# Linear attention in two-batch or one-batch units, ahead of a top-1 mixture of experts and a feed-forward layer

## The chip, the cores and the metric

One core of a Trainium2 chip runs the whole program. The metric is the device time of one execution in microseconds (us). The core's engines are TensorE (PE, matmuls; its weight loads are PEld), VectorE (DVE), ScalarE (ACT), GpSimd (POOL) and SyncE (SP, which here issues DMAs). Each works through its own queue in program order and waits on semaphores; transfers run on 16 DMA engines.

## The reference, cut to what matters

```python
# q, k, v: (8 batches, 8 heads, 576 positions, 64), f32
q_s = exp(q - max(q, axis=-1));  q_s = q_s / (sum(q_s, axis=-1) + 1e-9)
k_s = exp(k - max(k, axis=2));   k_s = k_s / (sum(k_s, axis=2) + 1e-9)   # axis 2: positions
kv  = einsum('bhsd,bhse->bhde', k_s, v)
x   = einsum('bhsd,bhde->bhse', q_s, kv)      # -> (4608 tokens, 512)
# then: x through one of 8 experts per token, picked by argmax(x @ w_gate):
#   gate * sigmoid(x @ w_output_gate) * (relu(x @ w1[e]) @ w2[e])
# then: h = x @ w_in;  out = (h * cos(h)) @ w_out
```

## The kernel before

The program has three stages: attention, the experts, the feed-forward layer. Only attention is touched.

Attention works in eight **units** w = 0 to 7 of four heads for two batches: unit w belongs to the pair of batches u = w // 2 and to its lower or upper four heads (n = w % 2). Lower partitions (0 to 63) hold the pair's first batch, upper ones (64 to 127) the second; a partition holds nine positions of each head, as `[128, 4 heads, 9, 64]`. Each of k, q and v is loaded by `load` in two DMAs, one for each half of the partitions (unit 0's k in four). All of them stand in SP's queue, with the stores of finished tiles (`xs`) between them. There are three buffers for k, two for q and two for v.

For k: VectorE takes the maximum over the nine positions in a partition (`k_max`, L368, two halves); TensorE transposes it (`k_T`), VectorE reduces again (`k_red`), TensorE spreads the result over the partitions (`k_bc`) and ScalarE copies it out (`k_cp`, tile bc). GpSimd subtracts it from k (`k_sub`, L393; unit 0 on VectorE), ScalarE takes the exponential (`k_exp`, L397), and TensorE multiplies k by v with a column of ones (`kv_mm`, L435). VectorE divides by the sum (`kv_fin`) into one of two tiles bd. From that, TensorE, with a transposition (`kv_T`) and a copy by ScalarE (`kv_cp`, tile bT, L456), works out the columns for the router's logits (`kv_w`, `kv_wc`).

For q: VectorE takes the maximum over 64 (`q_max`, L408), GpSimd subtracts it in place (`q_sub`, L412), and ScalarE takes the exponential into a tile e of the pair, `[128, 9, 8 heads, 64]` (`q_exp`, L418). There are two buffers of e; a pair's exponential waits until the last tile of two pairs ago has been transposed.

A pair has nine **tiles** i of 128 tokens, 36 in all. For each, TensorE transposes e (`x_T`, L473), ScalarE copies the result out of PSUM (`x_cp`, L477, tile qT), TensorE multiplies by bd (`x_mm`, L485), and ScalarE copies the product out in two pieces (`x_st`, L492 and L493). After each third tile VectorE takes reciprocals (`x_rec`), GpSimd scales the logits (`x_lt`, L508), VectorE sums them (`x_lg`), and SP stores the three tiles into xs. After nine tiles VectorE finds each token's expert (`argmax`, L520 to L528) and gate (`gate`).

When 27 tiles are done, the tokens for the first expert are ranked (`rank_cnt` to `first_idx`) and gathered from xs by GpSimd (L280), scaled, transposed (`trans0`, L627) and split into a high and a low part (`xhigh` L297, `xlow` L302). Meanwhile the first expert's weights are loaded (tile raw), cast by ScalarE (wh, L267) and subtracted (wl, L271) into space that attention's loads held until then. The first expert product is L1171.

`keep_clock` (L211) issues matmuls whose result nobody reads, at five places: at the start (30), ahead of the first k-v product (16), of the first expert's number (16), of the ranking (20), and ahead of the two transpositions in `trans0` (26 and 30).

What sets the order: `issue` gets each step with a key and the steps it depends on, and writes out the ready step with the least key. The key is a base time plus a number from the table `SHIFT`, one number a step and unit.

Of the kernel before, what the change touches and what calls it, by code (L numbers as in the profile page):

```python
# [60 lines left out]
def kernel(  # L61
# [21 lines left out]
    NT = N // 128  # L83
# [221 lines left out]
    with ExitStack() as actx:  # L305
# [34 lines left out]
        KEEP = {("kv", 0): 16, ("first",): 16, ("rk0",): 20}  # L340
# [4 lines left out]
        def hpair(m):  # L345
            return slice(2 * m, 2 * m + 2)

# [7 lines left out]
        def load(nm, pool, src, w):  # L355
            u, n = w // 2, w % 2
            t = V[nm, w] = pool.tile([128, HH, C, D], F32, tag=nm, name=nm)
            parts = 1 if w or nm != "k" else 2
            for m in range(parts):
                hs = slice(HH // parts * m, HH // parts * (m + 1))  # L360
                for b in range(2):
                    sy.dma_start(out=t[64 * b:64 * b + 64, hs], in_=src[2 * u + b, HH * n:HH * n + HH, :, :][hs].rearrange(
                        "h (p c) d -> p h c d", c=C))

        def k_max(w, m):
            if ("m1", w) not in V:
                V["m1", w] = ap2.tile([128, HH, D], F32, tag="m1", name="m1")
            ve.tensor_reduce(out=V["m1", w][:, hpair(m)], in_=V["k", w][:, hpair(m)].rearrange("p h c d -> p h d c"), axis=AX, op=ALU.max)  # L368
# [58 lines left out]
        def kv_mm(w, m):  # L427
# [3 lines left out]
            for c in range(C):  # L431
                for o in range(2):
                    for b in range(2):
                        pr = slice(64 * b, 64 * b + 64)
                        pe.matmul(kvp(w)[64 * o:64 * o + 64, b, m, :], V["k", w][pr, 2 * m + o, c, :], v1t[w % 2][pr, 2 * m + o, c, :],  # L435
# [22 lines left out]
        def kv_w(w):  # L458
            for b in range(2):
                for m in range(2):  # L460
                    for o in range(2):
                        pr = slice(64 * o, 64 * o + 64)
                        pe.matmul(kvw(w)[pr, b, m, :], V["bT", w][:, b, m, pr], wgo[:, HH * (w % 2) + 2 * m + o, :], start=True, stop=True)
# [11 lines left out]
        def x_cp(i):  # L475
            t = V["qT", i] = ap3.tile([128, NP, 128], F32, tag="qT", name="qT")
            sc.copy(out=t, in_=V["qp", i])  # L477

        def x_mm(i):
            xp = V["xp", i] = ps_x.tile([128, 2, NP, 128], F32, tag="x", name="xp")  # L480
            for j in range(NP):
                for o in range(2):
                    for b in range(2):
                        pr, rows = slice(64 * o, 64 * o + 64), slice(64 * b, 64 * b + 64)
                        pe.matmul(xp[rows, o, j, 0:BD], V["qT", i][pr, j, rows], bdt[i // C % NBD][pr, b, j, :], start=True, stop=True)  # L485

        def x_st(i, u):
# [4 lines left out]
            sc.copy(out=V["xt", i - u][:, u, :, 0:2 * D].rearrange("p j (o d) -> p o j d", o=2), in_=xp[:, :, :, 0:D])  # L492
            sc.copy(out=V["xl", i - u][:, u].rearrange("p j o g -> p o j g"), in_=xp[:, :, :, D:BD])  # L493
# [126 lines left out]
        def trans0(a):  # L620
# [4 lines left out]
            keep_clock(t.rearrange("p d c -> p (d c)"), (26, 30)[a])  # L625
# [20 lines left out]
        for w in range(NW):  # L646
# [9 lines left out]
            o("ldq", -8, lambda w=w: load("q", qp, q, w), ("qexp0", w - QB), ("qexp1", w - QB))  # L656
# [11 lines left out]
            for m in range(2):  # L668
                o(f"qsub{m}", 10 + 2 * m, lambda w=w, m=m, en=en: q_sub(w, m, en[f"qsub{m}"]), ("qmax", w))
# [1121 lines left out]
```

## Time and profile before

| | |
|---|---|
| median of 3 runs | 1466.26 us (1463.46 to 1467.59) |
| profiled execution | 1464.81 us |
| its span | 1462.6 us |
| TensorE busy | 1377.8 us (94%) |
| VectorE busy | 944.5 us (65%) |
| ScalarE busy | 860.6 us (59%) |
| GpSimd busy | 542.8 us (37%) |
| first expert product (L1173) | at 216.07 us of the span |

The profile gives, for one execution, what each engine did in each stretch of the span, what ended each idle time, and the chain of work that ended last. A busy share is a mean over stages, so the stretch that the change touches has to be asked for by itself. Times inside the span count from its start; 2.2 us of the profiled time lie outside it.

### The profile page before, as it was taken

What the parts mean: (1) busy time and instruction counts of PE and PEld (TensorE: products, weight loads), DVE (VectorE), ACT (ScalarE), POOL (GpSimd) and SP (SyncE); (2) the same over time, 40 slices, a digit from 0 to 9 for tenths busy, and PEclk for the clock granted to TensorE, in tenths of its full rate; (3) what the DMA queues carried; (4) which work ended last, traced back from release to release, by engine and by line L of the source; (5) the groups of instructions that cost most, each with busy time, mean ns of one, the idle gap of its engine ahead of it and who ended that gap; (6) DMA issues with size and microseconds to landing.
All of it is one profiled execution on the core that took longest, in us unless ns stands there. A gap on an engine that the chain in (4) does not pass through costs nothing.

```text
span 1462.6 us, 27860 instructions
## 1 busy us (share of the span) xinstructions
PE 1377.8 (94%) x10855; PEld 1223.6 (84%) x10855; DVE 944.5 (65%) x1415; ACT 860.6 (59%) x1561; POOL 542.8 (37%) x385
## 2 busy tenths in 40 slices
PE   4667589999999999999999999999999999999998
PEld 3455479899998999898898888988889898898986
DVE  5568659677887788876655655546565554655543
ACT  2456533555665656566766656666666666666654
POOL 3465532564635454625152423406042240603000
PEclk7588779999999999999999999999999999999999
DMA  9998533777988788897667675766667566665662
GB/s 207 222 247 216 176 125 123 250 254 255 343 283 300 269 282 296 280 315 251 219 188 217 175 229 167 213 191 195 207 168 232 171 203 201 196 203 171 205 177 82
DMA packets 164748, 318.15 MB, mean 218 GB/s; under 512 B 15040, under 2 KB 22720, under 8 KB 164608
## 3 DMA queue, kind: packets, MB, share of 16 engines
q1 hardware_dynamic: 133952, 263.12, 60.0%
q10 hardware_dynamic: 24656, 33.33, 6.2%
q0 software_dynamic: 6000, 19.83, 4.2%
q8 instruction: 88, 1.44, 0.4%
q14 instruction: 52, 0.43, 0.1%
HBM read 264.17 MB, written 52.05 MB: 216 GB/s over the span
## 4 chain that ended last, share of the span: by engine, by line
PE 83%; DVE 6%; DMA 5%; ACT 4%; issue 2%; SPq 0%; ACTq 0%; DVEq 0%
PE acc L1662 8%; PE acc L1660 8%; PE acc L1661 8%; PE bank L1596 7%; PE bank L1598 7%; PE bank L1597 7%; PE hp L1171 6%; PE hp L1174 6%; PE yps L1209 5%; PE yps L1208 5%; PE yps L1207 5%; PE hp L1173 4%; DMA k<-in_k_dram 2%; DMA v<-in_v_dram 2%; DVE n L1630 1%
## 5 line engine op out<-in xcount | busy, mean ns | idle before, releaser
L1596 PE MATMUL bank<-xo,wp 128*128 128x256 f32 x994 | 281.4, 283 | 2.1 <-ACT part L1610 0.6
L1597 PE MATMUL bank<-xo,wp 128*128 128x256 f32 x994 | 277.2, 279 | 0.6 <-DVE xo L887 0.6
L1598 PE MATMUL bank<-xo,wp 128*128 128x256 f32 x994 | 277.4, 279 | 0.0
L1639 DVE SCALAR_TENSOR_TENSOR n<-n,h 128x512 f32<-128x512 f32 x144 | 125.9, 874 | 171.3 <-ACT n L1636 171.3
L1660 PE MATMUL acc<-wh,ht 128*128 128x512 f32 x576 | 227.6, 395 | 0.4 <-ACT ht L1645 0.4
L1661 PE MATMUL acc<-wl,ht 128*128 128x512 f32 x576 | 227.4, 395 | 0.0
L1662 PE MATMUL acc<-wh,ht 128*128 128x512 f32 x576 | 226.8, 394 | 0.2 <-DVE ht L1649 0.2
L1596 PEld LDWEIGHTS bank<-xo,wp 128*128 128x128 f32 x994 | 186.8, 188 | 23.1 <-ACT part L1610 4.2
L1597 PEld LDWEIGHTS bank<-xo,wp 128*128 128x128 f32 x994 | 186.7, 188 | 17.1 <-DVE xo L887 0.8
L1171 PE MATMUL hp<-xTh,wh 128*128 128x256 f32 x704 | 190.6, 281 | 0.5 <-ACT xTh L297 0.5
L1174 PE MATMUL hp<-xTh,wl 128*128 128x256 f32 x704 | 188.8, 278 | 0.0
L1598 PEld LDWEIGHTS bank<-xo,wp 128*128 128x128 f32 x994 | 187.3, 188 | 0.0
L271 DVE TENSOR_TENSOR wl<-raw,wh 128x1024 fp32r<-128x1024 f32 x121 | 171.6, 1448 | 13.1 <-ACT wh L267 12.3
L887 POOL TENSOR_TENSOR xo<-x,xo 128x512 fp32r<-128x512 f32 x24 | 31.2, 1298 | 372.7 <-ACT xo L882 372.7
L1618 DVE TENSOR_TENSOR h<-bank,part 128x256 f32<-128x256 f32 x213 | 89.1, 420 | 110.6 <-PE bank L1598 109.8
L267 ACT CAST wh<-raw 128x1024 fp32r<-128x1024 f32 x126 | 126.8, 1051 | 54.5 <-PE yps L1209 35.7
L1173 PE MATMUL hp<-xTl,wh 128*128 128x256 f32 x544 | 151.5, 278 | 0.3 <-DVE xTl L302 0.3
L1625 ACT ACTIVATE n<-h 128x512 int32<-128x512 f32 x144 | 91.1, 633 | 101.9 <-DVE h L1618 98.1
L1633 ACT ACTIVATE n<-n 128x512 f32<-128x512 f32 x144 | 91.2, 633 | 77.4 <-DVE n L1630 77.3
L1171 PEld LDWEIGHTS hp<-xTh,wh 128*128 128x128 f32 x704 | 132.3, 188 | 1.8 <-ACT xTh L297 0.6
L1174 PEld LDWEIGHTS hp<-xTh,wl 128*128 128x128 f32 x704 | 132.2, 188 | 0.2
L1662 PEld LDWEIGHTS acc<-wh,ht 128*128 128x128 f32 x576 | 108.3, 188 | 26.3 <-DVE ht L1649 1.0
(290 smaller groups left out, 2977.6 us busy)
## 6 DMA issues: line engine op xcount, KB each, us to landing
wp<-ws SPq DMA_DIRECT2D x504, 256.0 KB, 2.8
raw<-in_moe_w_dram SPq DMA_DIRECT2D x60, 1024.0 KB, 7.5
ws<-wst ACTq DMA_DIRECT2D x28, 512.0 KB, 4.6
ys<-yt ACTq DMA_DIRECT2D x39, 256.0 KB, 4.8
xs<-xt SPq DMA_DIRECT2D x12, 780.0 KB, 5.0
v<-in_v_dram SPq DMA_DIRECT2D x16, 576.0 KB, 15.9
q<-in_q_dram SPq DMA_DIRECT2D x16, 576.0 KB, 13.2
out_dram<-o SPq DMA_DIRECT2D x35, 256.0 KB, 2.9
```

The costliest lines, as they stand in the source:

```text
L267: sc.copy(out=wh[j, c][:, s], in_=rawt[c][:, s])
L271: eng.tensor_tensor(out=wl[j, c][:, s], in0=rawt[c][:, s], in1=wh[j, c][:, s], op=ALU.subtract)
L1171: pe.matmul(hp[:, f2, :], w_h, xTh[j][:, d, :], start=(d == 0), stop=False)
L1173: pe.matmul(hp[:, f2, :], w_h, xTl[j][:, d, :], start=False, stop=False)
L1174: pe.matmul(hp[:, f2, :], w_l, xTh[j][:, d, :], start=False, stop=(d == KD - 1))
L1596: pe.matmul(h, w[:, 0, k], x[:, i, 0, k], start=(first and k == 0), stop=False, skip_group_check=True)
L1597: pe.matmul(h, w[:, 0, k], x[:, i, 1, k], start=False, stop=False, skip_group_check=True)
L1598: pe.matmul(h, w[:, 1, k], x[:, i, 0, k], start=False, stop=(k == 1), skip_group_check=True)
L1639: ve.scalar_tensor_tensor(out=rs[j, s], in0=rs[j, s], scalar=-0.5, in1=hs[j, s], op0=ALU.add, op1=ALU.mult)
L1660: pe.matmul(acc[t, a], gh[f][:, ts], w_h, start=(c == 0), stop=False)
L1661: pe.matmul(acc[t, a], gh[f][:, ts], w_l, start=False, stop=False)
L1662: pe.matmul(acc[t, a], gl[f][:, ts], w_h, start=False, stop=(c == KF - 1))
```

## The change

A unit w is now one batch with all its eight heads. Lower partitions hold its even heads, upper ones its odd heads; a pair u still has two units, its two batches. Since heads follow each other in memory, `load` now moves a unit with one DMA over all 128 partitions (unit 0's k with two). The four slots j of a unit are its four pairs of heads, and half m of a unit is the slots m and m + 2 (`spair`), so that columns of e, rows of bd and the logits' weights are picked in a new pattern; the tiles in xs are the same rows and columns as before.

`q_exp` goes. `q_sub` writes its difference into e, and `x_cp` takes the exponential while it copies the transposed tile out of PSUM. So the wait for a free e, which was ScalarE's, is GpSimd's.

`keep_clock` loses the 16 and the 20 ahead of the first expert's number and of the ranking; the 26 and 30 become 10 and 10. All numbers in `SHIFT` for attention are new.

```diff
-        KEEP = {("kv", 0): 16, ("first",): 16, ("rk0",): 20}
+        KEEP = {("kv", 0): 16}
...
+        def spair(m):
+            return slice(m, HH, 2)
...
         def load(nm, pool, src, w):
-            u, n = w // 2, w % 2
             t = V[nm, w] = pool.tile([128, HH, C, D], F32, tag=nm, name=nm)
+            rows = src[w].rearrange("h s d -> (h s d)").rearrange("(j p f) -> p j f", p=128, f=C * D)
             parts = 1 if w or nm != "k" else 2
             for m in range(parts):
-                hs = slice(HH // parts * m, HH // parts * (m + 1))
-                for b in range(2):
-                    sy.dma_start(out=t[64 * b:64 * b + 64, hs], in_=src[2 * u + b, HH * n:HH * n + HH, :, :][hs].rearrange(
-                        "h (p c) d -> p h c d", c=C))
+                js = slice(m, HH, parts)
+                sy.dma_start(out=t[:, js].rearrange("p j c d -> p j (c d)"), in_=rows[:, js])
...
         def q_sub(w, m, eng):
-            t = V["q", w][:, hpair(m)]
-            eng.tensor_tensor(out=t, in0=t, in1=V["qm", w][:, hpair(m)].unsqueeze(3).to_broadcast([128, 2, C, D]), op=ALU.subtract)
-
-        def q_exp(w, m):
             u, n = w // 2, w % 2
             if ("e", u) not in V:
                 V["e", u] = (ep if u % 2 else rp1).tile([128, C, H, D], F32, tag="e", name="e")
-            sc.activation(out=V["e", u].rearrange("p c h d -> p h c d")[:, HH * n + 2 * m:HH * n + 2 * m + 2], in_=V["q", w][:, hpair(m)],
-                          func=AF.Exp)
+            out_ = V["e", u].rearrange("p c h d -> p h c d")[:, HH * n + 2 * m:HH * n + 2 * m + 2]
+            eng.tensor_tensor(out=out_, in0=V["q", w][:, spair(m)], in1=V["qm", w][:, spair(m)].unsqueeze(3).to_broadcast([128, 2, C, D]),
+                              op=ALU.subtract)
...
-            sc.copy(out=t, in_=V["qp", i])
+            sc.activation(out=t, in_=V["qp", i], func=AF.Exp)
...
-            keep_clock(t.rearrange("p d c -> p (d c)"), (26, 30)[a])
+            keep_clock(t.rearrange("p d c -> p (d c)"), (10, 10)[a])
...
-            xl1={(0,): 55.71},
+            xl1={(0,): 49.31},
```

How the change moves instructions is shown at three places. Tiles carry their numbers there, so that two of one name can be told apart.

SP's queue at the start, before (each row an issue with the partitions and sizes of its target):

```order
L362 DMA k_215<-in_k_dram 64x2x576 x4
L362 DMA v_223<-in_v_dram 64x4x576 x2
L362 DMA q_231<-in_q_dram 64x4x576 x2
L362 DMA k_301<-in_k_dram 64x4x576 x2
L362 DMA v_326<-in_v_dram 64x4x576 x2
L362 DMA q_331<-in_q_dram 64x4x576 x2
```

and of the change:

```order
L364 DMA k_215<-in_k_dram 128x2x576 x2
L364 DMA q_224<-in_q_dram 128x4x576
L364 DMA k_238<-in_k_dram 128x4x576
L364 DMA v_261<-in_v_dram 128x4x576
L364 DMA q_267<-in_q_dram 128x4x576
L364 DMA k_274<-in_k_dram 128x4x576
```

Each pair of issues has become one, and q comes ahead of v.

GpSimd's queue around the units 5 to 7, before (L393 subtracts from k, L412 from q, L508 scales logits):

```order
L412 TENSOR_TENSOR q_953<-q_953,qm_1175 128x1152 x2
L543 IOTA ci_1242 128x512
L544 IOTA cj_1243 128x512
L393 TENSOR_TENSOR k_844<-k_844,bc_1125 128x1152 x2
L508 TENSOR_TENSOR xl_1129<-xl_1129,xt_1128 128x24x16
L412 TENSOR_TENSOR q_1290<-q_1290,qm_1454 128x1152 x2
L508 TENSOR_TENSOR xl_1281<-xl_1281,xt_1280 128x24x16
L393 TENSOR_TENSOR k_1042<-k_1042,bc_1623 128x1152 x2
```

and of the change (L394 subtracts from k, L416 from q into e):

```order
L416 TENSOR_TENSOR e_910<-q_1132,qm_1134 128x2x9x64
L416 TENSOR_TENSOR e_1410<-q_1263,qm_1265 128x2x9x64
L508 TENSOR_TENSOR xl_1144<-xl_1144,xt_1143 128x24x16
L394 TENSOR_TENSOR k_1007<-k_1007,bc_1515 128x2x576 x2
L508 TENSOR_TENSOR xl_1303<-xl_1303,xt_1302 128x24x16
L508 TENSOR_TENSOR xl_1414<-xl_1414,xt_1413 128x24x16
L394 TENSOR_TENSOR k_1581<-k_1581,bc_1701 128x2x576
L508 TENSOR_TENSOR xl_1663<-xl_1663,xt_1662 128x24x16
```

The first write into the last pair's e (e_1410) now stands ahead of both subtractions from the k of the units 6 and 7.

ScalarE's queue from the last exponential of k on, before (L267 casts expert weights, L456 copies bT, L477 copies a transposed tile):

```order
L397 ACTIVATE k_1354<-k_1354 128x1152
L267 CAST wh_2126<-raw_2112 128x1024
L267 CAST wh_2131<-raw_2124 128x1024 x2
L196 ACTIVATE d_2146<-d_2146 128x72
L201 ACTIVATE s_2151<-s_2151 128x9
L477 COPY qT_2184<-qp_1993 128x512
L267 CAST wh_2191<-raw_2129 128x1024 x2
L477 COPY qT_2208<-qp_2186 128x512
L477 COPY qT_2215<-qp_2210 128x512
L456 COPY bT_2246<-bp_2241 64x512
```

and of the change:

```order
L398 ACTIVATE k_1581<-k_1581 128x2x576
L267 CAST wh_2081<-raw_2060 128x1024
L267 CAST wh_2084<-raw_2072 128x1024 x2
L267 CAST wh_2081<-raw_2060 128x1024
L454 COPY bT_2102<-bp_2076 64x512
L475 ACTIVATE qT_2171<-qp_1985 128x512
L267 CAST wh_2195<-raw_2074 128x1024 x2
L475 ACTIVATE qT_2199<-qp_2173 128x512
L475 ACTIVATE qT_2206<-qp_2201 128x512
```

bT moved from behind five casts, the gate's two exponentials and three tiles to behind four casts.

## Rows read from the trace of the kernel before

**Rows 1.** The page's 40 equal slices of the span: busy share of the DMA engines in tenths.
```profile
DMA  9998533777988788897667675766667566665662
```

**Rows 2.** Stretches: length, each engine's busy us (instructions), granted clock, DMA share, GB/s.
```profile
10.00:40.00 30.00, 11.59 (x179) 8.25 (x179) 16.43 (x15) 7.51 (x8) 10.79 (x5) 0.68 1.05 222
40.00:70.00 30.00, 20.64 (x345) 16.31 (x346) 14.33 (x14) 13.85 (x21) 13.26 (x6) 0.56 1.05 222
234.00:240.00 6.00, 6.00 (x28) 4.93 (x27) 5.62 (x18) 0.95 (x3) 0.01 (x1) 1.00 1.05 396
```

**Rows 3.** DMA issues up to 216 us: count, KB each, median us to landing.
```profile
v<-in_v_dram SPq DMA_DIRECT2D x16, 576.0 KB, 15.9
q<-in_q_dram SPq DMA_DIRECT2D x16, 576.0 KB, 13.2
k<-in_k_dram SPq DMA_DIRECT2D x14, 576.0 KB, 15.7
...
k<-in_k_dram SPq DMA_DIRECT2D x4, 288.0 KB, 5.1
```

**Rows 4.** Waits up to 216 us: total us, times, longest.
```profile
DVE qm L408 <- DMA q<-in_q_dram: 20.3, 6, 5.5
...
ACT v L402 <- DMA v<-in_v_dram: 13.1, 2, 7.3
DVE m L368 <- DMA k<-in_k_dram: 12.9, 7, 2.6
```

**Rows 5.** Stretches again (PE, PEld, DVE, ACT, POOL busy; clock, DMA share, GB/s).
```profile
4.90:171.40 166.50, 107.67 (x2408) 85.99 (x2406) 108.58 (x144) 83.32 (x140) 84.47 (x46) 0.75 0.91 214
100.00:130.00 30.00, 20.85 (x564) 16.68 (x563) 28.08 (x42) 23.66 (x42) 18.65 (x11) 0.94 0.89 216
100.00:160.00 60.00, 43.45 (x1151) 34.95 (x1150) 50.59 (x68) 40.67 (x75) 40.57 (x22) 0.89 0.85 228
171.40:216.10 44.70, 31.96 (x463) 25.80 (x463) 23.29 (x78) 18.69 (x37) 16.79 (x12) 0.73 0.47 161
216.10:1462.60 1246.50, 1236.79 (x7982) 1110.87 (x7982) 809.89 (x1180) 757.29 (x1383) 439.87 (x317) 1.00 0.69 220
```

**Rows 6.** Groups by line up to 215 us: busy us, mean ns, idle before.
```profile
L393 POOL TENSOR_TENSOR k<-k,bc 128x1152 f32<-128x1152 f32 x14 | 36.9, 2657 | 18.8 <-ACT bc L389 18.5 <-DMA q<-in_q_dram 0.3
L412 POOL TENSOR_TENSOR q<-q,qm 128x1152 f32<-128x1152 f32 x16 | 35.2, 2217 | 28.2 <-DVE qm L408 21.5 <-ACT e L418 5.0 <-DVE rk L443 1.7
...
L477 ACT COPY qT<-qp 128x512 f32<-128x512 f32 x36 | 21.3, 592 | 16.2 <-PE qp L473 16.1
...
L418 ACT ACTIVATE e<-q 128x1152 f32<-128x1152 f32 x16 | 18.6, 1177 | 2.9 <-POOL q L412 2.9
...
L402 ACT COPY v<-v 128x1152 f32<-128x1152 f32 x7 | 8.0, 1157 | 13.1 <-DMA v<-in_v_dram 13.1
...
L267 ACT CAST wh<-raw 128x1024 fp32r<-128x1024 f32 x6 | 6.1, 1045 | 9.9 <-DMA raw<-in_moe_w_dram 9.9
```

**Rows 7.** The chain of waits, last part before the first expert product: start, us, what.
```profile
171.45 5.04 DMA raw<-in_moe_w_dram
...
188.15 0.59 ACT bT L456
...
206.83 3.29 PE t L211 x26
...
210.56 3.68 PE t L211 x30
```

**Rows 8.** Instructions in order of time on VectorE and GpSimd: start, us, what.
```profile
154.66 5.28 POOL L393 TENSOR_TENSOR k<-k,bc 128x1152 f32<-128x1152 f32 x2
...
154.91 2.56 DVE L523 TENSOR_TENSOR eq<-eq,rev 128x72 f32<-128x72 f32 x1
...
170.04 0.23 DVE L523 TENSOR_TENSOR eq<-eq,rev 128x72 f32<-128x72 f32 x1
...
209.78 1.05 POOL L285 TENSOR_TENSOR xg<-xg 128x512 f32<-128x512 f32 x1
```

More of the change, by code (lines that the diff above doesn't have):

```diff
@@ L462, in kv_w @@
                         pr = slice(64 * o, 64 * o + 64)
[L463 removed]
+                        pe.matmul(kvw(w)[pr, b, m, :], V["bT", w][:, b, m, pr], wgo[:, 4 * o + 2 * m + b, :], start=True, stop=True)
         def kv_wc(w):
@@ L476, in x_cp @@
             t = V["qT", i] = ap3.tile([128, NP, 128], F32, tag="qT", name="qT")
-            sc.copy(out=t, in_=V["qp", i])
+            sc.activation(out=t, in_=V["qp", i], func=AF.Exp)
         def x_mm(i):
[L480 to L485, printed above, removed]
+            xp = V["xp", i] = ps_x.tile([128, NP, 2, 128], F32, tag="x", name="xp")
+            for a in range(2):
+                for m in range(2):
+                    for o in range(2):
+                        for b in range(2):
+                            pr, rows = slice(64 * a, 64 * a + 64), slice(64 * b, 64 * b + 64)
+                            pe.matmul(xp[rows, 2 * a + m, o, 0:BD], V["qT", i][pr, 2 * b + m, 64 * o:64 * o + 64],
+                                      bdt[i // C % NBD][pr, o, 2 * b + m, :], start=True, stop=True)
         def x_st(i, u):
@@ L491, in x_st @@
             xp = V["xp", i]
-            sc.copy(out=V["xt", i - u][:, u, :, 0:2 * D].rearrange("p j (o d) -> p o j d", o=2), in_=xp[:, :, :, 0:D])
-            sc.copy(out=V["xl", i - u][:, u].rearrange("p j o g -> p o j g"), in_=xp[:, :, :, D:BD])
+            sc.copy(out=V["xt", i - u][:, u, :, 0:2 * D].rearrange("p j (o d) -> p j o d", o=2), in_=xp[:, :, :, 0:D])
+            sc.copy(out=V["xl", i - u][:, u], in_=xp[:, :, :, D:BD])
         def x_logits(i):
@@ L706 @@
         right = ("ldk", "ldv", "ldq", "kT", "kmax0", "kmax1", "kbc", "kcp", "ksub0", "ksub1", "kexp0", "kexp1",
-                 "v0", "v1", "qmax", "qsub0", "qsub1", "qexp0", "qexp1", "kv0", "kv1", "first")
-        op(PERIOD * 8 + 2, ("sw", 0), swap_pools, *[n for n in ops if n[0] in right or n[0] == "xT" and n[1] < NE])
+                 "v0", "v1", "qmax", "qsub0", "qsub1", "kv0", "kv1", "first")
+        op(PERIOD * 8 + 2, ("sw", 0), swap_pools, *[n for n in ops if n[0] in right or n[0] == "xT" and n[1] < NT - C])
         e0 = PERIOD * 8 + 3
@@ L835 @@
-            xst={('0', 0): -1.01, ('0', 1): -1.61, ('0', 2): -1.41, ('0', 3): 7.59, ('0', 4): 5.38, ('0', 5): 6.78, ('0', 6):
[5 rows of a table removed]
+            argmax={(0,): 17.32, (1,): 31.32, (2,): 25.32, (3,): 27.72},
+            fi={(0,): 31.32},
+            first={(0,): 16.32},
+            fm={(0,): 32.92},
+            gat={(0,): 44.71, (1,): 44.11},
+            gate={(0,): 37.72, (1,): 38.52, (2,): 38.12},
+            kT={('0',): -2.8, ('1',): -11.21, ('2',): -12.82, ('3',): -19.63, ('4',): -15.24, ('5',): -12.85, ('6',): -8.46,
+                ('7',): 9.14},
```

181 lines of the change are left out of this document (85 added, 96 removed), and 40 rows, old and new, of tables (xT, xcp, xmm, xst).

## The prediction

> **What bounds the kernel now.** I read the profile from the outside in. First the time slices: the DMA engines are full in the first three or four of 40 and never again for so long [rows 1]. The change lies in the first six only: attention, ending when the first expert product starts at 216.1 us. From there to the end, 1246.5 us, TensorE is busy for 1236.8 at full clock [rows 5]. That part is the same code in the same order, so it moves as a block: every microsecond by which the first product comes earlier is one off the end, and nothing else is.
>
> Inside the 216 us I asked which wait ends last. From 10 to 70 us the DMA engines are full (share 1.05) and yet move only 222 GB/s [rows 2]. Those bytes are loads of q, k and v: 46 issues of 576 KB and 4 of 288 [rows 3], 28.3 MB. At 222 GB/s they take 28.3 MB / 222 GB/s = 127.5 us. VectorE waits 20.3 us for q and 12.9 for k, ScalarE 13.1 for v [rows 4]. VectorE is only 65% filled up to the last k-v product (108.6 of 166.5 us) but 94% from 100 to 130 us and 84% from 100 to 160 [rows 5]. So the loads bound about 130 us, and a chain of 44.7 us from the last k-v product at 171.4 us to the first expert product ends the stage.
>
> **The change part by part.**
>
> *Loads over 128 partitions.* The same bytes in the same 2304-byte pieces, in 25 issues for 50. What differs is the span of partitions that one transfer writes: 64 before, 128 now. The trace has a load over 128 partitions alone in flight, an expert weight at 234 to 240 us: a share of 1.05 again, but 396 GB/s [rows 2]. I take that: 28.3 MB / 396 GB/s = 71.5 us. Bounds: 222 (no gain) and 396. [...]
>
> *What is late next.* VectorE's work before the last k-v product: maxima, v copies, sums, argmax and gates are the same instructions with the same sizes, 108.6 us [rows 5]. Its first input, two heads of k, now comes as one transfer; I leave its start at 4.9 us. Filled without a gap, the last k-v product would end at 4.9 + 108.6 = 113.5 us. Its fill decides: 94% is what it does when loads have run ahead, 84% is the mean of a stretch that mixes such time with waits for other engines, and 75% is the 84 minus again as much as it lies under 94. I take 84%: 4.9 + 108.6/0.84 = **134 us**, for 171.4 before, **37 us earlier**. At 94% it is 120, at 75% 150.
>
> *Queries' exponential.* 16 ScalarE instructions of 1.177 us go, 18.8 us; the 36 copies out of PSUM become exponentials. For one size (128x1152) an exponential takes 1177 ns and a copy 1157, so a PSUM copy of 592 ns stays at 590 to 605, at most 0.4 us over 36 [rows 6]. ScalarE is busy 83.3 of 166.5 us [rows 5], so I count the 18.8 at nothing; they shorten the way from q to its transposition by one instruction of 1.2 us a unit, which is in the fill.
>
> *GpSimd writes the difference straight into e.* Its inputs are the same; the output now goes to 64-element runs 2 KB apart. The trace has no such write on GpSimd. The nearest rows are the same subtraction in place (2.22 us) and k's (2.66) [rows 6]; a gain is excluded, since it reads as many elements as before. I take 2.22; 2.66 costs 16 x 0.44 = 7 us on an engine that is busy 84.5 of 166.5 us [rows 5], 91.5 of the 134 then: hidden, and not hidden only if the k-v product came before 100 us. A new wait comes with it: e has two buffers, so the subtraction waits until TensorE has transposed the last tile of two pairs ago. That wait was ScalarE's; now the scaling of xl and the subtractions from the k of units 6 and 7 stand behind it on GpSimd, and k's exponential and product wait for those. Before, GpSimd waited 5.0 us for it at second hand, behind ScalarE's exponential [rows 6]; nothing to 10 us, twice that, are the ends. I take nothing, since the 84% already holds waits of this kind.
>
> *Order and last chain.* Before, the product at 171.4 frees a buffer, expert weights land 5.04 us later, ScalarE casts them and waits, and only then copies bT at 188.15 [rows 7]; the last logits and nine tiles wait for that copy. It came 16.7 us after the product. Now bT stands behind the fourth cast: 5.04 + three casts of 1.05 [rows 6] = 8.2 us, then bT: **8.5 us earlier**. But only one tile is transposed ahead by then instead of three, and two transpositions more lie in the serial stretch (1.1 us on TensorE each): **2 us back**. The idle matmuls ahead of the two transpositions fall from 26 and 30 to 10 and 10. They took 3.29 + 3.68 us on the path [rows 7]; 20 of them take 2.5, which leaves 4.5, but the second transposition cannot start before its input is scaled at 209.78 + 1.05 [rows 8], 3.4 us ahead of where it now starts: **3.4 us earlier**. The 36 idle matmuls dropped elsewhere fill TensorE's waits; nothing. Sum: 44.7 - 8.5 + 2 - 3.4 = **34.8 us**, 9.9 less.
>
> **Sum.** First expert product at 134 + 34.8 = 169, for 216.1: 47 us earlier. The profiled execution took 1464.81 us, so 1417.8; it lies 1.45 under the median of the runs, which is inside their spread. I say **1418**. At 94% fill: 120 + 34.8 = 155, 61 earlier, 1404; at 75%: 184.5, 32 earlier, 1433.
>
> **Rivals.**
>
> *TensorE becomes the bound (chance 0.14).* [...]
>
> *VectorE and GpSimd get in each other's way (0.12).* The same 128x72 product took 2.56 us while GpSimd subtracted, and 0.23 when GpSimd stood idle [rows 8]. GpSimd's work is now squeezed from 166 us into some 130, so more of VectorE's two-input instructions meet it. About 15 such stand ahead of the last product; if seven more are caught it costs 7 x 2.33 = 16 us: (108.6 + 16)/0.84 + 4.9 = 153, product at 188, 1437. [...]
>
> *The loads don't get faster (0.08).* If 222 GB/s is the limit of the source or of 2304-byte pieces, the k-v product stays near 171 and only the last chain gains: 1455 at 9.9 us. The weight load at 396, in pieces of 2 KB, speaks against it.
>
> *Slower (0.03).* GpSimd's strided write. Up to the last k-v product GpSimd has 84.5 us of work; begun at 4.9 us at the earliest, it ends the stage later than now only if the product comes after 171.4 + 9.9 = 181, that is from (181 - 4.9 - 84.5)/16 = 5.7 us more per subtraction, 7.9 for 2.2. At 9 us each it is 4.9 + 84.5 + 16 x 6.8 = 198, first expert product at 233, **1482**. The slowest kind of subtraction in the rows is 2.66 [rows 6], so this is far.
>
> **How the numbers follow.** Forecast 0.63, TensorE 0.14, contention 0.12, loads 0.08, slower 0.03. Time: the forecast's, 1418. Range: 94% fill and a little more, 1398, to the two rivals at 1433 and 1437 with the 10 us of the e wait on top, 1446; outside are the loads, the slower case and the forecast's lowest edge, some 0.17. About 0.3% (4.4 us) is what a measurement of this kernel tells from no change. Faster: 0.63 + 0.14 + 0.12 + 0.06 of the loads case = 0.95; same 0.02, the rest of it; slower 0.03.
>
> **What would show it.** Right: between 10 and 40 us some 350 GB/s or more at a full share, or less with gaps; q's last load landing before 110 us; VectorE's waits for k and q under 10 us in all; the last k-v product at 120 to 150 and the first expert product 30 to 40 us behind it; 1246 us after that. Wrong: a full share at 222 GB/s; GpSimd's subtraction of q over 3 us, with k's exponential waiting for GpSimd; a clock near 0.56 through the stage with TensorE hardly idle; VectorE's 128x72 products at 2 us all through; a block after the first product that is not 1246 us long.

## The result, and the profile after

The changed kernel takes 1428.22 us (median of 4 runs, 1425.8 to 1431.1), the kernel before 1464.86 (4 runs, 1462.83 to 1467.59): a ratio of 0.9749, 95% interval 0.9723 to 0.9776. That is 36.6 us less; 1418 was predicted, 47 less, with a range of 1398 to 1446. The profiled execution took 1425.8 us, the quickest of the four, with a span of 1424.0.

The page's DMA slices answer to [rows 1]: the engines are no longer full four slices long.

```profile
DMA  9855437679896979886675666756666575665652
```

Stretches of the changed kernel (length, busy us and instructions of PE, PEld, DVE, ACT and POOL, granted clock, DMA share, GB/s), against [rows 2, 5]. In order: the loads; the attention up to the last k-v product, now at 133.40 us; the last chain from there to the expert products (L1169, at 177.97, as L1173 before; a lone product of L1167, L1171 before, stands about 1 us ahead of it); the block behind it; and then the last chain in its three parts, cut where ScalarE starts to copy bT and where the last tile's product ends.

```profile
10.00:40.00 30.00, 19.14 (x378) 14.17 (x376) 27.51 (x25) 11.10 (x14) 20.16 (x9) 0.72 1.01 380
40.00:70.00 30.00, 24.80 (x766) 21.32 (x764) 26.77 (x28) 20.95 (x40) 27.50 (x14) 1.00 0.86 315
4.90:133.40 128.50, 99.11 (x2391) 81.64 (x2388) 106.14 (x135) 66.73 (x124) 85.22 (x47) 0.84 0.74 268
133.40:177.97 44.57, 30.86 (x409) 25.54 (x406) 21.65 (x86) 18.64 (x37) 14.78 (x11) 0.66 0.50 179
177.97:1424.00 1246.03, 1237.56 (x7982) 1111.28 (x7982) 809.61 (x1181) 756.67 (x1383) 437.71 (x318) 1.00 0.67 221
133.40:141.80 8.40, 0.64 (x7) 0.46 (x5) 2.02 (x9) 2.83 (x3) 2.62 (x2) 0.84 0.72 251
141.80:171.90 30.10, 25.96 (x371) 21.95 (x371) 15.70 (x64) 13.88 (x31) 9.34 (x7) 0.53 0.45 161
171.90:178.00 6.10, 4.29 (x35) 3.15 (x33) 3.96 (x13) 1.93 (x4) 2.82 (x3) 1.00 0.46 173
```

The same three parts of the last chain before the change (the stretches are cut at a tenth of a us, so the tables below can differ by 0.1):

```profile
171.40:188.20 16.80, 7.32 (x43) 5.57 (x43) 7.69 (x27) 5.94 (x10) 6.97 (x3) 0.70 0.49 172
188.20:206.80 18.60, 16.22 (x352) 13.47 (x353) 9.87 (x35) 10.71 (x24) 5.07 (x4) 0.63 0.40 131
206.80:216.10 9.30, 8.42 (x73) 6.76 (x69) 5.73 (x16) 2.04 (x5) 4.75 (x5) 1.00 0.56 200
```

Read together they place the gain, for these two executions. Loads: 380 GB/s for 222 at nearly the same share. Last k-v product: 171.4 to 133.4, 38.0 us earlier. Last chain: 44.7 and 44.6, nothing gained. Block: 1246.5 and 1246.0. Sum 38.0 + 0.1 + 0.5 = 38.6, the difference of the spans. Inside the last chain two parts did what was forecast (16.8 to 8.4, 9.3 to 6.1) and the middle one took it back: the last nine tiles need 30.1 us for 18.6.

Waits of the changed kernel up to 134 us (total, times, longest), against [rows 4, 6]: the waits for q and k are down to 1.5 us in all, and GpSimd has one of 14 us for TensorE's transposition, the one that came with e.

```profile
DVE qm L409 <- DMA q<-in_q_dram: 0.9, 1, 0.9
DVE m L369 <- DMA k<-in_k_dram: 0.6, 1, 0.6
...
POOL e L416 <- PE qp L471: 15.2, 2, 14.1
```

Groups by line, against [rows 6] (busy us, mean ns, idle before): GpSimd's strided write and ScalarE's exponential out of PSUM.

```profile
L416 POOL TENSOR_TENSOR e<-q,qm 128x1152 f32<-128x1152 f32 x16 | 34.2, 2149 | 24.2 <-PE qp L471 15.2 <-DVE qm L409 9.0
...
L475 ACT ACTIVATE qT<-qp 128x512 f32<-128x512 f32 x36 | 21.7, 602 | 28.0 <-PE qp L471 28.0
```

### The profile page after: what moved, and what is told of

Read it like the earlier page. It is cut to its first block, busy times and chain, and to the rows that moved or that the text cites. A ratio compares the mean times of both kernels' runs of the same rounds, so it can differ in the third digit from the quotient of the medians.

```text
span 1424.0 us, 27631 instructions
## 1 busy us (share of the span) xinstructions
PE 1368.9 (96%) x10783; PEld 1219.4 (86%) x10783; DVE 940.1 (66%) x1415; ACT 843.3 (59%) x1545; POOL 539.4 (38%) x385
## 5 line engine op out<-in xcount | busy, mean ns | idle before, releaser
L1167 PE MATMUL hp<-xTh,wh 128*128 128x256 f32 x704 | 190.7, 281 | 0.0
L267 ACT CAST wh<-raw 128x1024 fp32r<-128x1024 f32 x126 | 127.0, 1050 | 54.7 <-PE yps L1205 31.8
L1169 PE MATMUL hp<-xTl,wh 128*128 128x256 f32 x544 | 151.7, 279 | 0.6 <-DVE xTl L302 0.6
L1167 PEld LDWEIGHTS hp<-xTh,wh 128*128 128x128 f32 x704 | 132.3, 188 | 1.0
```

Of the source, the lines that this page charges most:

```text
L267: sc.copy(out=wh[j, c][:, s], in_=rawt[c][:, s])
L1167: pe.matmul(hp[:, f2, :], w_h, xTh[j][:, d, :], start=(d == 0), stop=False)
L1169: pe.matmul(hp[:, f2, :], w_h, xTl[j][:, d, :], start=False, stop=False)
```

## The experiments

Each kernel but e11 is the changed one with the edit shown. The table puts the last chain of each profiled execution in its three parts; "product" is the end of the last k-v product. The ratio is to the kernel before, timed on the same chip, so two kernels are best compared by their ratios (0.001 is 1.5 us).

| kernel | median us | ratio (95%) | product | to bT | nine tiles | to expert product |
|---|---|---|---|---|---|---|
| before | 1464.86 | 1 | 171.4 | 16.8 | 18.7 | 9.2 |
| changed | 1428.22 | 0.9749 (0.9723 to 0.9776) | 133.4 | 8.4 | 30.1 | 6.1 |
| e1 loads in halves | 1470.23 | 1.0053 (1.0036 to 1.0071) | 175.1 | 8.0 | 29.6 | 6.1 |
| e2 exponential on ScalarE | 1444.94 | 0.9876 (0.9843 to 0.9910) | 150.4 | 8.3 | 29.4 | 6.1 |
| e3 idle matmuls in the gap | 1426.83 | 0.9752 (0.9729 to 0.9775) | 133.5 | 9.8 | 27.3 | 6.1 |
| e4 bT first | 1421.94 | 0.9720 (0.9694 to 0.9746) | 138.1 | 1.6 | 28.1 | 6.5 |
| e5 extra exponentials | 1430.33 | 0.9764 (0.9746 to 0.9782) | 140.1 | 8.3 | 26.0 | 7.0 |
| e6 idle matmuls back | 1432.94 | 0.9774 (0.9749 to 0.9798) | 140.4 | 9.5 | 33.4 | 9.2 |
| e7 subtraction later | 1426.36 | 0.9744 (0.9717 to 0.9771) | 135.6 | 8.5 | 27.4 | 6.4 |
| e8 clock held | 1421.68 | 0.9700 (0.9675 to 0.9725) | 138.3 | 1.6 | 28.5 | 6.1 |
| e9 halves alternate | 1422.13 | 0.9717 (0.9698 to 0.9737) | 133.6 | 8.1 | 24.7 | 6.5 |
| e10 e9 with bT first | 1414.34 | 0.9670 (0.9654 to 0.9686) | 132.1 | 1.6 | 26.3 | 6.1 |
| e11 before, halves grouped | 1474.65 | 1.0070 (1.0048 to 1.0093) | 173.6 | 16.8 | 24.3 | 9.9 |
| e12 as e2, placed later | 1438.35 | 0.9837 (0.9819 to 0.9855) | 142.8 | 8.2 | 31.0 | 7.2 |

### e1: the loads in halves

```diff
-                sy.dma_start(out=t[:, js].rearrange("p j c d -> p j (c d)"), in_=rows[:, js])
+                for b in range(2):
+                    pr = slice(64 * b, 64 * b + 64)
+                    sy.dma_start(out=t[pr, js].rearrange("p j c d -> p j (c d)"), in_=rows[pr, js])
```

> The changed kernel, but every load of q, k and v is written as two transfers of 64 partitions each, of the same bytes in the same 2304-byte pieces. My theory (the span of partitions was the limit, and the 38 us by which the last k-v product came earlier are the loads'): 10 to 40 us show about 222 GB/s at a full share as before the change, the last k-v product ends at 160 to 172 us for 133.4, and the time is 1455 to 1466 us. The rival (the new order and the exponential out of PSUM made the gain, the loads were hidden): the k-v product stays within 10 us of 133.4 and the time under 1440.

Two stretches of e1:

```profile
10.00:40.00 30.00, 10.79 (x187) 7.23 (x189) 19.31 (x16) 4.72 (x6) 13.61 (x6) 0.70 1.05 222
...
4.90:175.10 170.20, 117.44 (x2391) 97.19 (x2388) 104.12 (x135) 67.02 (x124) 83.76 (x47) 0.72 0.87 204
```

222 GB/s again to the digit, the product at 175.1 us, and 1470 us: 3 and 4 over the upper ends that the theory gave. The bytes, the pieces and the rest of the change are the same. But e1 also has twice the transfers, of half the size, and a smaller transfer is a rival for the 222. Unit 0's k settles it. The changed kernel loads it first, in two transfers of 576 KB over 128 partitions, the size of e1's later ones over 64. From 3 to 5 us, in which the changed kernel has not moved all of these two (0.87 of 1.18 MB by 5 us), it and e1 show:

```profile
3.00:5.00 2.00, 1.44 (x7) 0.91 (x7) 1.45 (x6) 0.48 (x1) 0.60 (x1) 1.00 1.08 362
...
3.00:5.00 2.00, 1.43 (x7) 0.88 (x7) 1.34 (x5) 0.46 (x1) 0.59 (x1) 1.00 1.01 243
```

So 576 KB over 128 partitions move at 362 GB/s, and the span of partitions of one transfer is what makes 222 or 380. By the ratios this part is worth 1.0053 - 0.9749 = 0.030, some 44 us. All else in the change, with slow loads, costs 8 us (0.5%).

### e2, e5 and e12: what the moved exponential is worth

e2 puts it back on ScalarE, into e (the main lines; the wait for e and the release of q's buffer go back to ScalarE with it):

```diff
-            out_ = V["e", u].rearrange("p c h d -> p h c d")[:, HH * n + 2 * m:HH * n + 2 * m + 2]
-            eng.tensor_tensor(out=out_, in0=V["q", w][:, spair(m)], ...
+            t = V["q", w][:, spair(m)]
+            eng.tensor_tensor(out=t, in0=t, ...
...
+            sc.activation(out=V["e", u].rearrange("p c h d -> p h c d")[:, HH * n + 2 * m:HH * n + 2 * m + 2],
+                          in_=V["q", w][:, spair(m)], func=AF.Exp)
...
-            sc.activation(out=t, in_=V["qp", i], func=AF.Exp)
+            sc.copy(out=t, in_=V["qp", i])
```

> The changed kernel, but the queries' exponential is again ScalarE's, out of q into e after GpSimd's subtraction in place, and the move out of PSUM is a copy again; everything else stays. It adds 16 ScalarE instructions of about 1.18 us (18.8 us) and takes the wait for a free e from GpSimd to ScalarE. My theory (the moved exponential is worth nothing, ScalarE being busy 67 of the 128 us ahead of the last k-v product): the last k-v product within 4 us of 133.4, the time 1425 to 1434. The rival (the exponential on the way from q to its transposition was part of what bounded the stage): k-v product at 140 or later, 1436 to 1450. A third: GpSimd's 14 us wait for e goes, k's subtraction of unit 6 starts 10 us earlier, and the time falls to 1418 to 1424.

e5 adds the same load to ScalarE with no tie to other work, at the same places (its main line; the note behind # is not in the kernel):

```diff
+            sc.activation(out=dum[0], in_=dum[0], func=AF.Exp, scale=0.0)   # for each of the 16 halves of q
```

> The changed kernel with 16 further exponentials of 128x1152 on ScalarE, on a scratch tile that nothing else reads or writes, at the places in ScalarE's order where the run with the exponential on ScalarE had them (and one memset of that tile at the start). They take 16 x 1.17 = 18.8 us of ScalarE and wait for nothing. With the exponential itself back on ScalarE the last k-v product came at 150.5 us for 133.4 and the time was 1445. Theory one (that was the order: ScalarE waited 13.3 us for GpSimd's subtractions in the middle of its queue, with the copies for the next unit's k and k-v behind; its busy time is hidden): k-v product within 5 us of 133.4, 1426 to 1433. Theory two (the busy time itself is on the path): k-v product at 143 or later, 1438 to 1447.

e12 is e2 with the exponentials further back in ScalarE's queue (against e2, the start of the line):

```diff
-                o(f"qexp{m}", 13 + 2 * m, ...
+                o(f"qexp{m}", 19 + 2 * m, ...
```

> The run with the exponential back on ScalarE, with every one of the 16 exponentials placed later in ScalarE's order by 6 units of its key, behind work that is ready earlier. With them close behind the subtractions ScalarE waited 13.3 us for GpSimd and the time was 1445; 16 exponentials without a tie cost 0 to 2 us. Theory one (only the place in the queue cost): ScalarE's wait for GpSimd's subtraction under 5 us and the time 1426 to 1436. Theory two (the longer way from q to the transposition, and the later release of q's buffers, cost wherever it stands): 1438 to 1450.

ScalarE's groups up to the last k-v product: the exponential in e2.

```profile
L419 ACT ACTIVATE e<-q 128x1152 f32<-128x1152 f32 x16 | 18.7, 1176 | 14.4 <-POOL q L413 13.3 <-PE qp L474 1.1
```

The extra ones in e5:

```profile
L423 ACT ACTIVATE dum<-dum 128x1152 f32<-128x1152 f32 x16 | 18.7, 1172 | 0.1
```

The exponential in e12, which waits for nothing:

```profile
L419 ACT ACTIVATE e<-q 128x1152 f32<-128x1152 f32 x16 | 18.4, 1173 | 0.0
```

In e12, TensorE now waits for the exponential (waits up to 150 us):

```profile
PE qp L474 <- ACT e L419: 7.3, 3, 3.2
```

and VectorE's work up to the product is larger (length, busy us of PE, PEld, DVE, ACT and POOL):

```profile
4.90:142.75 137.85, 100.06 (x2391) 80.60 (x2388) 113.81 (x135) 82.92 (x140) 86.31 (x47) 0.85 0.69 250
```

**e5.** The 18.7 us of ScalarE by themselves cost 2 us of the time, and the interval meets the changed kernel's. Theory one holds by the time, but not by the product, which came 6.7 us later for the 5 allowed; the nine tiles, 26.0 us for 30.1, made up for it in that execution.

**e2.** The same 18.7 us with their ties cost 17 us by the medians and 19 by the ratios, all of it ahead of the product (150.4 for 133.4). ScalarE stood 13.3 us for GpSimd, with copies for other units behind, while VectorE's work stayed (107.1 us for 106.1). So my theory, no loss, is wrong and its rival holds; the third, a gain, is out.

**e12.** Here ScalarE stood for nothing and TensorE waited instead, and the loss is 10 us by the medians and 13 by the ratios. Theory two's time holds, just (1438.35 of 1438 to 1450). Its reason isn't shown: VectorE's 135 instructions took 113.8 us for 106.1, which at the same fill of 83% makes most of the 9.4 us by which the product came later. Why they took longer wasn't asked; meeting more of GpSimd's, the prediction's second rival, is one possibility.

So what e2 lost wasn't ScalarE's time but its place on the way from q to its transposition, and for e12 that stays open. The later release of q's buffer explains little: VectorE waits 0.8 us for q in e2 and 3.7 in e12, for 0.9. Both orders are the changed kernel's with one kind of step put in; whether an order made for the exponential on ScalarE would cost less wasn't tried, so the 10 to 13 us are an upper bound of what the move is worth.

### e3 and e8: the clock in the last nine tiles

```diff
-        KEEP = {("kv", 0): 16}
+        KEEP = {("kv", 0): 16, ("kvT", 7): 44}
...
+            keep(t.rearrange("p b m c -> p (b m c)"), "kvT", w)
```

> The changed kernel with 44 idle matmuls put ahead of the four transpositions behind the last k-v product, into the 7 us in which TensorE stands idle until ScalarE has copied bT (134.9 to 142.4 us); nothing else moves. My theory (the nine last tiles take 30.1 us from bT to their last product, for 18.7 before, because TensorE runs at half its clock from 142 to 170 us after that idle time): the granted clock stays near 1.0 behind bT, the tile stretch falls to 19 to 23 us, the time to 1417 to 1421. The rival (the order of the tiles makes TensorE wait for ScalarE's move of each transposition, whatever the clock): the stretch stays at 27 to 30 us and the time at 1425 to 1431.

Two stretches of e3, from the last k-v product to bT and from bT to the last tile's product:

```profile
133.40:143.20 9.80, 5.99 (x52) 4.74 (x49) 2.97 (x10) 2.80 (x3) 3.71 (x2) 1.00 0.81 270
143.20:170.60 27.40, 22.36 (x371) 18.85 (x371) 15.59 (x64) 13.83 (x31) 9.37 (x7) 0.69 0.42 149
```

The idle matmuls kept the clock at 1.00 while they ran, and it fell all the same: they end at 138.95 us, TensorE stands from 139.4 to 143.9, until bT is there, and the tiles' products take 1.95 us up to 154.5. The stretch is 2.8 us shorter and bT 1.4 later; by the ratios nothing is gained. The edit doesn't do what it was meant to, so it doesn't decide.

e8 tried it again on top of e4 (below; against e4):

```diff
-        KEEP = {("kv", 0): 16}
+        KEEP = {("kv", 0): 16, ("fm",): 12}
...
+            keep(t, "fm")
...
-            wh={... (2, 0): 31.55, (2, 1): 31.0},
+            wh={... (2, 0): 38.0, (2, 1): 41.5},
```

> The kernel with bT ahead of the casts, and two more edits in the stretch of the last nine tiles: 12 idle matmuls ahead of the 27 small products that sum the rows of the first expert, and ScalarE's last two casts moved from ahead of the fifth tile's move to behind the sixth's and eighth's. In that kernel the tiles' products took 1.12 us each up to 153 us and 1.95 from 157 on, after TensorE had stood idle for most of 153.3 to 156.9. Theory one (TensorE's granted clock sets the length of the stretch): it stays near 1.0, the stretch from bT to the last product falls from 28.1 to 18 to 23 us, and the time from 1422 to 1413 to 1418. Theory two (ScalarE's moves and casts set it): the stretch stays over 26 us and the time within 2 us of 1422.

A stretch of e8's tiles:

```profile
152.00:156.00 4.00, 3.81 (x82) 3.57 (x84) 2.79 (x12) 1.26 (x3) 0.63 (x1) 0.50 0.00 2
```

Theory two's numbers came, 28.5 us and 1421.68. But the clock was at the lower level (0.50) from 144 us on, before the idle matmuls (157.9 us) were reached (it is at 1.00 from 160 on), so this fails to test it, too. That the level matters follows from the products alone: 1.95 us at 0.50, 1.12 at 1.00 (changed kernel, below). A way to keep it up wasn't found.

### e4: bT ahead of the casts

```diff
-            kvcp={... ('7',): 29.03}
+            kvcp={... ('7',): 25.1}
...
-            xcp={... ('3', 6): 19.12,
+            xcp={... ('3', 6): 8.87,
...
-            wh={(0, 0): 19.52, (0, 1): 21.12, (1, 0): 16.92, (1, 1): 15.32, (2, 0): 25.11, (2, 1): 23.51},
+            wh={(0, 0): 19.52, (0, 1): 32.8, (1, 0): 29.8, (1, 1): 28.6, (2, 0): 31.55, (2, 1): 31.0},
```

> The changed kernel with ScalarE's order altered at one place: the copy of bT and the move of the first transposed tile stand ahead of the five casts that wait for expert weights, and these casts stand between the moves of the last tiles. My theory: bT comes at about 135.2 us for 141.8, the tiles start 6.5 us earlier, and TensorE idles 1 us for 7, so its clock stays up: 6.5 us from the start and up to 10 from the clock, 1412 to 1422. Rival one (the clock falls anyhow, the casts take ScalarE's time between the tiles): 3 to 7 us, 1421 to 1425. Rival two (the ranking and the wait for the scaled gathers set the end): no gain, 1425 to 1431.

ScalarE's instructions there, in order of time (start, us), of the changed kernel:

```profile
138.97 2.94 ACT L267 CAST wh<-raw 128x1024 fp32r<-128x1024 f32 x3 [7.04 <-DMA raw<-in_moe_w_dram]
...
141.81 0.57 ACT L454 COPY bT<-bp 64x512 f32<-64x512 f32 x1
```

and of e4:

```profile
139.70 0.58 ACT L454 COPY bT<-bp 64x512 f32<-64x512 f32 x1 [3.21 <-PE bp L450]
```

In the changed kernel bT waits behind casts that wait 7.04 us for weights; in e4 it follows the product by 1.6 us for 8.4. The last chain is 36.2 us for 44.6. This execution's k-v product came 4.7 us later than that of the changed kernel, which has the same order up to there (the last section shows where they part), so the two profiled executions differ by 3.6. By the medians the gain is 6 us, by the ratios 4, with intervals that meet. That is what rival one gave: the start came earlier, and the nine tiles still took 28.1 us. The clock fell to the lower level within them (0.70 on average), and ScalarE's casts stand between their moves; what each of the two costs isn't separated.

### e6: the idle matmuls back

```diff
-        KEEP = {("kv", 0): 16}
+        KEEP = {("kv", 0): 16, ("first",): 16, ("rk0",): 20}
...
-            keep_clock(t.rearrange("p d c -> p (d c)"), (10, 10)[a])
+            keep_clock(t.rearrange("p d c -> p (d c)"), (26, 30)[a])
```

> The changed kernel with the idle matmuls of before put back: 16 ahead of the first expert's product, 20 ahead of the ranking counts, 26 and 30 for 10 and 10 ahead of the two transpositions of the gathered rows. My theory: those ahead of the ranking stand behind bT now and are on the path (20 at 0.13 to 0.25 us: 2.5 to 5 us), those ahead of the transpositions cost the 3.4 us that I counted; less what a clock that rises earlier in the tile stretch gives back (0 to 5 us): 1429 to 1436. The rival (their removal let the clock fall and cost the 10 us that were missing): 1416 to 1422.

e6's 20 idle matmuls (start, us) in the last chain:

```profile
150.50 4.96 PE L211 MATMUL rk<-lc,tri 128*128 128x288 bf16 x20 [8.55 <-ACT bT L454]
```

3.1 us more from the last tile to the expert product (9.2 for 6.1), and 5 us ahead of the first of the last tiles, since in the new order the 20 stand behind bT. So dropping them took 8 us out of the chain; by the ratios the whole time is 4 us longer with them, with intervals that meet. The rival, that their removal let the clock fall and cost the missing 10 us, is out: the time didn't fall.

### e7: GpSimd's wait for e

```diff
-            qsub1={... ('6',): -4.86,
+            qsub1={... ('6',): 5.6,
```

> The changed kernel with one of GpSimd's subtractions into e, the first of unit 6, moved behind unit 6's two subtractions from k. In the changed kernel GpSimd stood 14.1 us at that place (79.6 to 93.6) until TensorE had transposed the last tile of two pairs ahead, with unit 6's k behind it. Theory one (that wait put off the last k-v product): unit 6's subtraction from k starts 3 us earlier, when the copy of its maxima lands at 96.0 at the latest, or up to 15 us earlier if that copy is moved by the same wait; the time falls by 2 to 12 us, 1416 to 1426. Theory two (k's own chain, the maximum, its transposition and copy at 96.3, is as late): within 2 us of 1428.

GpSimd's waits in e7 up to 134 us:

```profile
POOL xl L508 <- DVE xt L504: 14.8, 1, 14.8
POOL k L394 <- ACT bc L390: 14.5, 4, 5.2
...
POOL e L416 <- PE qp L471: 0.4, 1, 0.4
```

The 14.1 us for e are gone, and the next instruction in the queue, the scaling of xl, waits 14.8 us for VectorE. Behind it, k's subtraction waits for the copy of its maxima. The time is 0.9744 against 0.9749, theory two: that wait alone bounded nothing, since another took its place.

### e9, e10 and e11: the order of a tile's 32 products

Two transpositions more, as I had counted, don't make 11.4 us, and e3 and e8 had left the clock open. So I compared TensorE's groups up to the first expert product (count, busy us, mean ns, idle before), before:

```profile
L485 PE MATMUL xp<-bd,qT 64*64 64x81 f32 x1152 | 37.5, 283 | 7.8 <-issue 6.2 <-ACT qT L477 0.7 <-DVE bd L466 0.7
```

and of the changed kernel:

```profile
L484 PE MATMUL xp<-bd,qT 64*64 64x81 f32 x1152 | 47.2, 272 | 11.0 <-ACT qT L475 8.1 <-issue 2.5 <-ACT xl L493 0.4
```

The same 1152 products take 9.7 us more, though the mean of one is no longer (272 ns for 283): they overlap less. One tile's 32 in order of time, before, at the lower level (granted clock 0.50) and at full clock (1.00):

```profile
193.40 1.36 PE L485 MATMUL xp<-bd,qT 64*64 64x81 f32 x32
...
201.07 0.80 PE L485 MATMUL xp<-bd,qT 64*64 64x81 f32 x32
```

and changed, likewise:

```profile
145.56 1.95 PE L484 MATMUL xp<-bd,qT 64*64 64x81 f32 x32
...
170.79 1.12 PE L484 MATMUL xp<-bd,qT 64*64 64x81 f32 x32 [0.75 <-ACT qT L475]
```

The change rewrote the loop nest of `x_mm`, with the layout of its tiles: the half of the partitions that both inputs are read from (o before, a now) was changed after every second matmul call, and is now the outermost loop. A tile has 16 such calls in the source, which the profile lists as 32 matmuls; so eight calls, 16 of the 32, in a row read one half. e9 changes that loop alone:

```diff
-            for a in range(2):
-                for m in range(2):
-                    for o in range(2):
+            for m in range(2):
+                for o in range(2):
+                    for a in range(2):
                         for b in range(2):
```

> The changed kernel with one loop nest written in another order: the 32 products of 64x64x81 of a tile go through the partition halves of their inputs (a) inside the loops over m and o, so that every second product changes half, as before the change; in the changed kernel a is the outermost loop, and 16 products in a row read the same half. Same products, same operands, same places in all queues. The 32 took 0.80 us at full clock and 1.36 at the lower level before, 1.12 and 1.95 in the changed kernel. My theory (the loop order alone makes that): 0.80 and 1.36 again; the last nine tiles take about 9 x 0.5 = 4 to 5 us less from bT to their last product, up to 27 x 0.32 = 8 us less ahead of the last k-v product; 1416 to 1424. The rival (the products' time comes from their operands' layout, or TensorE is not what the tiles wait for): 1.12 and 1.95 stay, or the time stays at 1426 to 1430.

e11 does the reverse to the kernel before:

```diff
-            for j in range(NP):
-                for o in range(2):
+            for o in range(2):
+                for j in range(NP):
                     for b in range(2):
```

> The kernel before the change with the same loop nest turned the other way: the half of the inputs (o) is the outermost loop, so that 16 products in a row read one half, as in the changed kernel. If the loop order makes the time of these products, 32 of them take 1.12 us at full clock and 1.95 at the lower level for 0.80 and 1.36, and the last chain grows by 3 to 5 us: the time 1464 to 1470 for 1463. If it is the layout: 0.80 and 1.36 stay and so does the time.

e9's group:

```profile
L484 PE MATMUL xp<-bd,qT 64*64 64x81 f32 x1152 | 35.5, 275 | 11.2 <-ACT qT L475 7.7 <-issue 3.0 <-ACT xl L493 0.4
```

and one of its tiles at the lower level:

```profile
145.51 1.36 PE L484 MATMUL xp<-bd,qT 64*64 64x81 f32 x32
```

e11's group:

```profile
L485 PE MATMUL xp<-bd,qT 64*64 64x81 f32 x1152 | 52.1, 289 | 4.9 <-issue 3.8 <-DVE bd L466 0.6 <-ACT qT L477 0.5
```

and one of its tiles, likewise:

```profile
196.20 1.95 PE L485 MATMUL xp<-bd,qT 64*64 64x81 f32 x32
```

Both ways the loop order makes the whole difference in a tile's products: 1.95 to 1.36 and 1.36 to 1.95, with the operands' layout untouched. The nine tiles fall from 30.1 to 24.7 in e9 and rise from 18.7 to 24.3 in e11. By the ratios it is worth 5 us in the changed kernel (the intervals just meet) and 10 in the one before, more than the 1464 to 1470 that I gave for e11. At the lower level 32 products take 1.36 us when they alternate and 1.95 when they mostly don't; what in TensorE makes that isn't shown.

Ahead of the last k-v product the 27 tiles' products are shorter, too, and there I had allowed up to 8 us. e9 up to its product:

```profile
4.90:133.62 128.72, 93.83 (x2391) 75.35 (x2388) 105.02 (x135) 66.69 (x124) 84.21 (x47) 0.83 0.74 268
```

TensorE has 5.3 us less work than in the changed kernel (93.8 for 99.1) at nearly the same clock, and the product comes at 133.6 for 133.4: in these executions TensorE's work isn't what it waits for.

e10 is e9 with e4's edit.

> The run before together with bT ahead of the casts. Theory one (two separate terms of the last chain, 4 to 5 us and 6 to 8): the last chain falls from 44.6 to 30 to 33 us and the time to 1410 to 1417. Theory two (with the tiles' products shorter, ScalarE's casts between the moves set the pace): no more than bT first alone, 1419 to 1423.

Two stretches of e10: up to the last k-v product, and the last chain.

```profile
4.90:132.05 127.15, 94.34 (x2391) 76.43 (x2388) 105.60 (x135) 66.77 (x124) 84.22 (x47) 0.81 0.76 271
132.05:166.10 34.05, 24.44 (x408) 19.39 (x407) 26.46 (x87) 18.21 (x37) 15.88 (x11) 0.75 0.71 233
```

The last chain is 34.05 us, 1 over what theory one gave, and the time 1414.34, inside it; the ratio of 0.967 (0.9654 to 0.9686) is clear of e4's and e9's. The two terms add, if not in full: the nine tiles take 26.3 us for e9's 24.7, with five of ScalarE's casts among them.

## Why the prediction was right, and where it was off

**Right, and shown by a run.** The loads were the bound, and the span of partitions was their limit (e1: 222 GB/s, 44 us given back). The block behind the first expert product moved as a block (1246.0 for 1246.5).

**Right, but not shown by a run: VectorE comes next.** It is busy 106.1 of 128.5 us, a fill of 83% where I took 84%, and the last k-v product came at 133.4 for 134. e9 speaks against TensorE's work as the bound, but no run made VectorE's work less. The closeness is partly luck: the same order gave 133 to 140 in other profiled executions, and this one was the quickest of its four. Two of my signs failed: the first expert product came 44.6 us behind the k-v product for the 30 to 40 that I named, and q's last load was issued at 108.0 us only, so that it landed after 110.

**Right in size.** bT came 8.4 us behind the product for 8.2 predicted. The last part of the chain lost 3.1 us for 3.4. The exponential out of PSUM takes 602 ns, inside 590 to 605. GpSimd's strided write takes 2.149 us for the 2.22 I took; that is a small gain, which I had excluded.

**Off: the tiles in the last chain, 2 us in the sum, 11.4 measured.** This is as large as the miss: 34.8 us predicted for the chain, 44.6 measured, while its other two parts were within 0.3. The step that failed is "two transpositions more lie in the serial stretch". TensorE's two largest groups in the nine tiles (busy us, mean ns, idle before), before the change, in the changed kernel and in e9:

```profile
L485 PE MATMUL xp<-bd,qT 64*64 64x81 f32 x288 | 10.2, 308 | 0.0
L473 PE MATMUL qp<-ident,e 128*128 128x128 f32 x20 | 5.1, 403 | 1.8 <-ACT qT L477 1.8
...
L484 PE MATMUL xp<-bd,qT 64*64 64x81 f32 x288 | 15.3, 333 | 1.7 <-ACT qT L475 1.7
L471 PE MATMUL qp<-ident,e 128*128 128x128 f32 x32 | 8.8, 428 | 1.6 <-ACT qT L475 1.6
...
L484 PE MATMUL xp<-bd,qT 64*64 64x81 f32 x288 | 9.8, 298 | 2.1 <-ACT qT L475 2.1
L471 PE MATMUL qp<-ident,e 128*128 128x128 f32 x32 | 7.9, 394 | 2.1 <-ACT qT L475 2.1
```

Of the 11.4 us, 5.1 are the products. I took them as unchanged, because their number and size are; the loop order was in the change and I didn't weigh it. In one tile it costs 0.32 us at full clock and 0.59 at the lower level, and with it put back (e9) they take 9.8 us, no more than before. Another 3.7 are the transpositions. I had counted three tiles transposed ahead of bT before; that is the number of moves, and a fourth tile stood transposed in PSUM (the transpositions start at 164.85, 182.53, 184.30 and 186.14 us). In the changed kernel there is one (131.01), so three more lie in the stretch: eight tiles of four matmuls (x32) for five (x20). The rest, 2.6, is some 0.9 of other small matmuls, mainly the ranking's that stood ahead of bT before, and 1.7 of waits. The clock is no separate cause of this size: it was 0.53 over the stretch for 0.63 before, but e9, with 0.65, still needs 24.7 us for 18.7. Those 6 us are neither loop nor clock; my count had 2 for them. Where the clock alone was higher, at 0.67 to 0.72 in the changed kernel's order of tiles (e3, e5, e7), the nine tiles took 26.0 to 27.4 us for 30.1, so it can be worth 3 to 4 us in an execution.

**Right sum, wrong reason: the exponential.** I counted its move at nothing, since ScalarE was half idle. By the time, the idle half does hide its work (e5, 2 us). But ScalarE's queue was one more on the way from q to TensorE, and with the exponential there the changed kernel is 10 to 19 us slower (e2, e12). I had said that this step is in the fill, and e2's loss is there; e12's goes with longer work of VectorE, whose cause isn't shown.

**A bound that was too narrow: the wait for e.** I gave nothing to 10 us; it took 15.2 in two waits. Taking nothing for its cost was right (e7).

**The rivals.** The TensorE rival is there in part: in some executions its clock falls at 50 us and the k-v product comes 2 to 8 us later (below). Its 1433 in the range takes a granted clock of 0.56 all the way to that product, which no run shows: where the clock fell to 0.50 and 0.52 from 50 to 60 us (e4, e6), its mean up to the product was 0.81 and 0.79, and the product ended at 138.1 and 140.4. VectorE's work up to the first expert product didn't grow, 127.8 us for 131.9, so contention with GpSimd cost no more than before in the changed kernel. GpSimd's own work stayed, 85.2 us for 84.5, so its write made nothing slower.

## What to carry to other kernels

A load that writes 64 partitions is worth making into one over 128 before anything else is tuned, if the loads bound the stage (here 380 GB/s for 222, and some 44 us). When a change rewrites a loop nest of small matmuls, look at which half of the partitions follows which: the count and the shapes can be the same and the time 40% longer (1.95 us for 1.36). A wait that is named in the profile may bound nothing (the 14.1 us for e, gone in e7), and an engine that is half idle may still be on the path (17 to 19 us in e2); take each away, one at a time.

## What the runs showed of the hardware that I had not expected

The order of small matmuls is worth nearly as much as the clock: 32 products of 64x64x81 took 0.80 us (halves alternating, before) and 1.12 (16 in a row from one half, changed) at a granted clock of 1.00, 1.36 and 1.95 at 0.50, so 1.4 times by the order and 1.7 by the clock.

Runs of one order part at one place. From 50 to 60 us, the changed kernel:

```profile
50.00:60.00 10.00, 8.58 (x275) 7.36 (x277) 8.87 (x9) 7.29 (x13) 8.99 (x4) 1.00 0.79 304
```

and e4, which doesn't differ from it up to there:

```profile
50.00:60.00 10.00, 9.85 (x117) 8.23 (x112) 6.63 (x7) 4.32 (x9) 3.73 (x2) 0.50 0.97 343
```

With the granted clock at 1.00 there (changed, e3, e9, e10) the last k-v product ended at 132.1 to 133.6 us; with 0.50 to 0.53 (e4, e6, e7, e8) TensorE was busy for 9.3 to 10.0 of the 10 us, and it ended at 135.6 to 140.4. The clock there isn't all: e5, with its extra exponentials, shows 1.00 and its product ended at 140.1. Why the clock falls in one execution and not in the next isn't shown: TensorE was busy 7.7 of the 10 us before in the one and 6.8 in the other.
